# A chunked recurrence with inverses from GpSimd: ten units prepared ahead in place of eight, inverses returned in parts

## The chip, the cores and the metric

One core of a Trainium2 chip runs the whole program. The metric is the time of one execution in microseconds of device time, the median of several runs. TensorE multiplies matrices (stationary operand loaded first, results into PSUM), VectorE, ScalarE and GpSimd work elementwise, and SyncE's queue issues transfers; ScalarE's queue issues some too. Each engine works through its own list of instructions in order, and so does each queue: an instruction that waits holds up everything behind it.

## The reference

Two blocks follow each other. The first is a recurrence over 768 steps for 4 batches x 8 heads with a 40x40 state, the second a mixture of 8 experts with a capacity of 80 tokens each:

```python
for t in range(S):                                   # S = 768, D = 40, 32 chains (B x H)
    y[:, :, t] = einsum('bhd,bhde->bhe', r_t, state)
    Sa = einsum('bhde,bhe->bhd', state, a_t)
    state = state * w_t[:, :, None, :] - einsum('bhd,bhe->bhde', Sa, b_t) + einsum('bhd,bhe->bhde', v_t, k_t)
x = y.transpose(0, 2, 1, 3).reshape(B * S, H * D)    # 3072 tokens x 320
logits = x @ w_gate; expert = argmax(logits); gate = softmax(logits)[expert]
for e in range(8):                                   # the 80 tokens with the largest gate of each expert
    out[tok] = gate[tok] * (relu(x[tok] @ w1[e]) @ w2[e])
```

Everything is float32; w1 is 320x1024 and w2 is 1024x320 per expert. Tokens that are not kept stay zero.

## The kernel before

**Units and groups.** The 768 steps are cut into 12 chunks of 64. A unit is one chunk of two batches (16 chains), so there are 24 units, and batch pair 0 has the even ones, pair 1 the odd ones. Four units make a group (GU = 4, six groups). For a unit the 64 steps are solved at once: with N the strictly triangular 64x64 matrix of scores of each chain, the inverse of (I - N) is needed.

**prepare(n)** (line 356) loads w, a, k and b of a unit and makes what does not need the state: running products P of w and their inverses iv by two scans on VectorE (L374, L382), the scaled ah and kb (L392, L412), the transposed keys kbT (eight transposes on TensorE at L423, copied by ScalarE at L427), and two scores by TensorE at L438: N, which ScalarE copies to nt (L451), and Psi, which VectorE masks to psi (L455). LOOK = 8 rings of P, ah, kb and psi let units be prepared eight ahead of the solve; nt has two groups' worth.

**invert(gi)** (line 465) inverts the N of a group. Each 64x64 triangle is two 32x32 triangles and a 32x32 block below. out_go (L478) writes the triangles of the four units to `blocks` in device memory, fetch (L489) reads them back so that each of 128 partitions holds one 32x32 triangle (tile lt). 30 steps of two instructions (L497, L499) invert it in place: on VectorE for the first group, on GpSimd for the other five. end (L506, L507) closes it, flip (L511, GpSimd) makes the transposed copy ltT, two transfers (L517) put both to `solved` and `flipped`, and back_go (L522) reads them into nt, d1 and d0, eight transfers. lt and ltT have one buffer each.

**solve(n) and finish(n)** (lines 536, 570): two joins on TensorE (L546, L561) with copies by ScalarE (L551, L566) fill the lower block of the inverse. finish loads r and v (r on ScalarE's queue), transposes them, and does the products with the state: psi x V (L636), state x ah (L665), the inverse x W (L683, VectorE masks at L688), the keys' products (L705), the new state (L716, L725) and the tokens (L729, L739). Unit n+2 needs the state that unit n leaves.

**gate(gi)** (line 753) ranks the tokens of a group on VectorE, ten rounds of L807 and L808.

**What sets the order.** Nothing is scheduled at run time. Every piece is given to a Plan (line 18) with an engine, a duration, a lag, a due time, and the names that it reads and writes. Plan.order takes, again and again, the ready piece that can start first (within SLACK), and among those the one with the smaller key, ALPHA times the due time less the longest chain behind it; it assigns PSUM banks on the way. The list that comes out is emitted in that order, engine by engine, and stays fixed.

After the last unit the tops are merged (L828 on), the expert weights are loaded into the memory that the first part held, the chosen tokens are gathered and the experts computed (lines 830 to 1001).

## Time and profile before

| | |
|---|---|
| median of 3 runs | 606.74 us (604.84 to 608.82) |
| the profiled execution | 603.29 us, of it span 601.3 us |
| busy in the span: TensorE, VectorE, GpSimd, ScalarE | 424.1, 344.8, 248.5, 171.1 us |
| first join of the first group starts | 94.12 us |
| last token product of the first part | 464.57 us |
| the ranked tops are complete, the expert part starts | 478.9 us |
| TensorE's granted clock, mean | 0.848 of full speed |

The profiled execution lies 3.45 us under the median of the runs. The first part, up to 478.9 us, is what the change touches; the expert part takes the remaining 122 us. A stretch of the timeline in which TensorE has next to no busy time is one in which the whole chain waits, since the products with the state are all on TensorE.

### The profile page before, as it was taken

What the parts mean: (1) busy time and instruction counts of PE and PEld (TensorE: products, weight loads), DVE (VectorE), ACT (ScalarE), POOL (GpSimd) and SP (SyncE); (2) the same over time, 40 slices, a digit from 0 to 9 for tenths busy, and PEclk for the clock granted to TensorE, in tenths of its full rate; (3) what the DMA queues carried; (4) which work ended last, traced back from release to release, by engine and by line L of the source; (5) the groups of instructions that cost most, each with busy time, mean ns of one, the idle gap of its engine ahead of it and who ended that gap; (6) DMA issues with size and microseconds to landing.
All of it is one profiled execution on the core that took longest, in us unless ns stands there. A gap on an engine that the chain in (4) does not pass through costs nothing. (4 is left out here: it accounts for less than half of the span.)

```text
span 601.3 us, 20521 instructions
## 1 busy us (share of the span) xinstructions
PE 424.1 (71%) x8878; PEld 334.9 (56%) x8878; DVE 344.8 (57%) x692; ACT 171.1 (28%) x323; POOL 248.5 (41%) x392
## 2 busy tenths in 40 slices
PE   2853387998079975898559994984397104799996
PEld 1743266896068864787548883873286004244443
DVE  9985963795538763887546880764543883112121
ACT  1431142454024451444214542332042000110100
POOL 9010021798359860599518981388100002201011
PEclk9995687998579996999778995997599555699999
DMA  6586568556854558565593428414500299990000
GB/s 100 93 129 111 91 151 141 104 100 100 186 110 75 114 122 153 123 125 92 136 186 78 93 66 169 81 31 84 122 15 4 54 388 383 336 341 15 7 15 14
DMA packets 238414, 72.74 MB, mean 121 GB/s; under 512 B 218100, under 2 KB 232692, under 8 KB 238324
## 3 DMA queue, kind: packets, MB, share of 16 engines
q1 hardware_dynamic: 211444, 65.85, 48.2%
q10 hardware_dynamic: 26112, 3.94, 4.2%
q0 software_dynamic: 768, 1.64, 0.9%
q8 instruction: 70, 1.15, 0.8%
q14 instruction: 20, 0.16, 0.1%
HBM read 53.26 MB, written 18.13 MB: 119 GB/s over the span
## 5 line engine op out<-in xcount | busy, mean ns | idle before, releaser
L497 POOL TENSOR_TENSOR tmp<-lt 128x30 f32<-128x30 f32 (+9 forms) x150 | 89.0, 593 | 91.7 <-DMA lt<-blocks 80.3
L499 POOL TENSOR_TENSOR lt<-lt,tmp 128x30 f32<-128x30 f32 (+9 forms) x150 | 95.1, 634 | 11.8
L546 PE MATMUL ps<-d,nt 128*64 128x64 f32 x384 | 21.6, 273 | 52.8 <-DMA d<-flipped 52.8
L688 DVE TENSOR_TENSOR UL<-ps,mask 128x832 f32<-128x832 f32 x24 | 24.5, 1019 | 46.6 <-PE ps L683 46.4
L546 PEld LDWEIGHTS ps<-d,nt 128*64 128x64 f32 x384 | 18.8, 183 | 54.4 <-issue 40.7
L986 POOL DMA_INDIRECT out_dram<-y,idx_s x8 | 7.4, 921 | 74.4 <-DVE y L985 74.4
L438 PE MATMUL ps<-ah,kbT 40*64 40x64 f32 x1536 | 32.4, 231 | 7.8 <-ACT kbT L427 7.3
L427 ACT COPY kbT<-ps 128x1024 f32<-128x1024 f32 x24 | 24.3, 1013 | 43.7 <-PE ps L349 23.5
L983 PE MATMUL yp<-w,hT 128*80 128x320 f32 x128 | 35.9, 433 | 0.5 <-DVE hT L976 0.5
L438 PEld LDWEIGHTS ps<-ah,kbT 40*64 40x64 f32 x1536 | 27.9, 143 | 13.3 <-ACT kbT L427 9.7
L349 PE MATMUL ps<-ident,raww 128*128 128x128 f32 x96 | 18.3, 322 | 21.8 <-DMA raww<-in_w_dram 21.8
L716 DVE TENSOR_TENSOR st<-ps,st 128x832 f32<-128x832 f32 (+1 forms) x24 | 23.9, 995 | 16.3 <-PE ps L705 15.8
L455 DVE TENSOR_TENSOR psi<-ps,mask 128x512 f32<-128x512 f32 x24 | 16.1, 681 | 29.8 <-PE ps L438 29.7
L382 DVE TENSOR_TENSOR_SCAN iv<-dec,ends 128x520 f32<-128x520 f32 x24 | 31.4, 1309 | 2.6 <-ACT ivc L401 1.3
L374 DVE TENSOR_TENSOR_SCAN P<-dec,begins 128x520 f32<-128x520 f32 x24 | 31.8, 1323 | 1.4 <-ACT dec L370 1.1
L960 PE MATMUL hp<-w,xe 128*80 128x512 f32 x64 | 31.8, 643 | 0.5 <-DVE xe L952 0.5
L349 PE MATMUL ps<-ident,kb 128*128 128x128 f32 x192 | 27.7, 289 | 5.5 <-DVE kb L412 5.1
L739 PE MATMUL ps<-wsel,xT 128*128 128x88 f32 x192 | 27.0, 284 | 5.0 <-DVE xT L729 5.0
L592 ACT COPY rv<-ps 128x1024 f32<-128x1024 f32 x24 | 24.3, 1013 | 19.7 <-DMA rawr<-in_r_dram 9.7
L739 PEld LDWEIGHTS ps<-wsel,xT 128*128 128x128 f32 x192 | 23.6, 194 | 7.5 <-DVE xT L729 6.1
L551 ACT COPY gt<-ps 128x256 f32<-128x256 f32 x24 | 9.0, 374 | 66.2 <-PE ps L546 65.2
L485 POOL MEMSET nt<- 32x1024 f32 x12 | 11.3, 944 | 38.9 <-ACT nt L451 38.5
(157 smaller groups left out, 955.9 us busy)
## 6 DMA issues: line engine op xcount, KB each, us to landing
w<-in_moe_w_dram SPq DMA_DIRECT2D x8, 1280.0 KB
w<-in_moe_w_dram SPq DMA_DIRECT2D x8, 1024.0 KB, 14.3
x_rows<-xg SPq DMA_DIRECT2D x24, 160.5 KB, 3.2
rawkb<-in_k_dram SPq DMA_DIRECT2D x48, 80.0 KB, 3.0
rawkb<-in_b_dram SPq DMA_DIRECT2D x48, 80.0 KB, 2.9
raww<-in_w_dram SPq DMA_DIRECT2D x48, 80.0 KB, 3.2
rawa<-in_a_dram SPq DMA_DIRECT2D x48, 80.0 KB, 3.4
rawr<-in_r_dram ACTq DMA_DIRECT2D x96, 40.0 KB, 3.0
```

The lines of the kernel that those rows point to most:

```text
L349: nc.tensor.matmul(o, lhsT=i, rhs=ident, start=True, stop=True, is_transpose=True, skip_group_check=True)
L374: nc.vector.tensor_tensor_scan(at("P", n), at("dec", n)[:, 0 : H * SEG], begins, 0.0, op0=Alu.mult, op1=Alu.add)
L382: nc.vector.tensor_tensor_scan(at("iv", n)[:, H * SEG : 0 : -1], at("dec", n)[:, H * SEG : 0 : -1], at("ends", n)[:, H * SEG : 0 : -1], 0. ...
L427: nc.scalar.copy(at("kbT", n).rearrange("p (k c) -> p k c", k=2), ps[:, bank(kk) : bank(kk) + 2, :])
L438: nc.tensor.matmul(ps[T * o : T * o + T, b0 + q, T * m : T * m + T], lhsT=at("kbT", n)[rows, s0 : s0 + T], rhs=chain(at("ah", n), rows, m, ...
L497: e.tensor_tensor(out=tv, in0=t3[:, 0:s, s : s + 1].to_broadcast([128, s, n]), in1=t3[:, s : s + 1, s + 1 :].to_broadcast([128, s, n]), op ...
L499: e.tensor_tensor(out=t3[:, 0:s, s + 1 :], in0=t3[:, 0:s, s + 1 :], in1=tv, op=Alu.add)
L546: nc.tensor.matmul(ps[HB * q : HB * q + HB, b0, T * i : T * i + T], lhsT=nt[:, q, i, :], rhs=d0[:, q, i, :], start=True, stop=True, skip_g ...
L688: nc.vector.tensor_tensor(out=view(at("UL", n), 0, (M4 * X, 2), (1, M4 * X)), in0=view(ps[:, bank(ku), :], 0, (512, 2), (1, M4 * X)), in1= ...
L739: nc.tensor.matmul(ps[:, b0, 88 * m : 88 * m + 88], lhsT=at("xT", n)[:, 2 * T * cof(m, 0) : 2 * T * cof(m, 0) + 2 * T], rhs=wsel[:, m, :], ...
L960: nc.tensor.matmul(hp[j], lhsT=xe[:, i, :], rhs=w1[:, i, FH * j : FH * j + FH], start=i == 0, stop=False)
L983: nc.tensor.matmul(yp, lhsT=hT[:, f, :], rhs=w2[:, f, :], start=f == 0, stop=f == FK - 1)
```

## The change

- **Depth.** LOOK goes from 8 to 10, nt from two groups to three, lt from one buffer to two; psi shrinks from 8 buffers to 2, VL (the v tile) from 3 to 2. N and Psi are separated: the transposed keys are made as two halves, bT in prepare and kT in the new make_psi(n), which stands at the unit's solve.
- **Joins on 32-row tiles.** L546 and L561 multiplied 128-row operands whose other halves are zeros. Now only the 32-row blocks are multiplied, 16 matmuls in place of 8 for each join, each half into a PSUM bank of its own. The returned tiles d0 and d1 become one compact tile d, with no zeros to fill; the two fills of 128x2048 on GpSimd go.
- **The return in parts.** back_go becomes d0_go, d1_go and tm_go, three pieces on SyncE's queue with their own names (d0, d1, tm), so the first join needs d0, the second d1, and only the product with the inverse (L683) needs tm. There are still eight transfers. The clear of nt now stands behind the four units' N copies by name.
- **The flip** of an inverse moves from GpSimd to ScalarE.
- **Front.** The strict masks are copied by ScalarE (four copies) in place of VectorE (eight); loads of `a` for units 0 to 5 go through ScalarE's queue; the zero fills of padding get names of their own, so that the first loads don't stand behind them.
- **Order.** SLACK 0.15 to 0.05, ALPHA 0.5 to 0.25, and some of the durations that the Plan is told change by a few per cent.

```diff
-SLACK = 0.15
+SLACK = 0.05
-ALPHA = 0.5
+ALPHA = 0.25
...
-    LOOK = 8
-    RINGS = dict(dec=2, ..., psi=LOOK, nt=2 * GU, VL=3, UL=1, iv=1, ivc=1, ends=1, kbT=1, rv=1, lt=1, ltT=1, d0=GU, d1=GU, ...
+    LOOK = 10
+    RINGS = dict(dec=2, ..., psi=2, nt=3 * GU, VL=2, UL=1, iv=1, ivc=1, ends=1, bT=1, kT=1, rv=1, lt=2, ltT=1, tm=3 * GU, d0=GU, d1=GU, ...
-    WIDE = dict(nt=2, d0=1, d1=1)
+    WIDE = dict(nt=(3, GU * 512), d=(1, GU * 256))
...
-        for name in ("d0", "d1"):
-            for i, t in enumerate(wide[name]):
-                fill("POOL", t, 0.0, [(name, GU * i + u) for u in range(GU)], 2.0, -800.0)
...
-                for o in (0, X, 2 * X + D, 3 * X + D):
-                    nc.vector.tensor_copy(mask[rows, o : o + T], strict[rows, T * bb : T * bb + T])
+                for o in (view(mask[rows], 0, (X, 2), (1, T)), view(mask[rows], 2 * X + D, (X, 2), (1, T))):
+                    nc.scalar.copy(o, strict[rows, T * bb : T * bb + T].unsqueeze(1).to_broadcast([T, 2, T]))
...
-            load("rawa", n, z - 12, [(a, rows4)])
+            load("rawa", n, z - 12, [(a, rows4)], (), "ACT" if n < 6 else "SP")
...
+            key_turn(n, "bT", 1, z + 5)
+            kn = ("N", n)
+            add("PE", 0.62, 0.2, z + 7, score(n, kn, "bT", lambda q, bb: bb ^ q), ...)
...
+        def make_psi(n):
+            z = n * PER - 5
+            kp = ("Psi", n)
+            key_turn(n, "kT", 0, z)
+            add("PE", 0.62, 0.2, z + 1, score(n, kp, "kT", lambda q, bb: bb), ...)
...
             def flip():
-                nc.gpsimd.tensor_copy(at("ltT", kq)...
+                nc.scalar.copy(at("ltT", kq)...
-            add("POOL", 2.0, 0.1, z + 4.1, flip, [lk], [("ltT", kq)])
+            add("ACT", 1.05, 0.2, z + 4.1, flip, [lk], [("ltT", kq)])
...
-            add("SP", 4.8, 2.2, z + 5, back_go, [("sol", kq), ("flp", kq)], [(name, n) for n in ns for name in ("d0", "d1", "nt")])
+            add("SP", 1.2, 2.5, z + 4.4, d0_go, [("flp", kq)], [("d0", n) for n in ns])
+            add("SP", 2.2, 2.5, z + 4.5, d1_go, [("sol", kq)], [("d1", n) for n in ns])
+            add("SP", 1.1, 2.5, z + 4.6, tm_go, [("sol", kq)], [("tm", n) for n in ns], to=[("nt", n) for n in ns])
...
                 for i in range(M4):
                     for q in range(2):
-                        nc.tensor.matmul(ps[HB * q : HB * q + HB, b0, T * i : T * i + T], lhsT=nt[:, q, i, :],
-                                         rhs=d0[:, q, i, :], ...)
+                        for x in range(2):
+                            rows = slice(T * x, T * x + C)
+                            nc.tensor.matmul(ps[HB * q + C : HB * q + HB, b0 + x, C * i : C * i + C], lhsT=nt[rows, q, i, C:],
+                                             rhs=d0[rows, q, i, :], ...)
...
                 solve(n)
+                make_psi(n)
                 finish(n)
```

The order that the Plan makes of it is a table too long to show. Three places follow; numbers behind names are buffers.

GpSimd's list at the end of the second group's inversion (its lt is buffer 0 before, buffer 1 after); first before, then the change:

```order
L497 TENSOR_TENSOR tmp_150<-lt_0_129 128x30
L499 TENSOR_TENSOR lt_0_129<-lt_0_129,tmp_150 128x30
L195 AFFINE_SELECT lt_0_129<-lt_0_129 128x1024
L507 MEMSET lt_0_129 128x32
L511 COPY ltT_0_130<-lt_0_129 128x1024
L787 TENSOR_TENSOR ids_59<-gsm_0_145,tok_157 128x32
L788 COPY og_0_143<-gates_58 128x4x8
L485 MEMSET nt_0_146 32x32x32 x2
L497 TENSOR_TENSOR tmp_150<-lt_0_129 128x30
```

```order
L499 TENSOR_TENSOR tmp_151<-lt_1_130 128x30
L501 TENSOR_TENSOR lt_1_130<-lt_1_130,tmp_151 128x30
L195 AFFINE_SELECT lt_1_130<-lt_1_130 128x1024
L509 MEMSET lt_1_130 128x32
L487 MEMSET nt_2_149 32x32x32 x2
L499 TENSOR_TENSOR tmp_151<-lt_0_129 128x30
```

Between two inversions there stand two closing instructions and one clear, and the next inversion works on the other lt; the flip is gone from this list, and the ids of the first group come later.

SyncE's queue at the return of the second group's inverse (`solved`, `flipped`), with the fetch of the third group's triangles (lt<-blocks); first before, then the change:

```order
L517 DMA solved<-lt_0_129 128x1024
L795 DMA x_rows<-xg_0_137 64x2x321 x4
L517 DMA flipped<-ltT_0_130 128x1024
L478 DMA blocks<-nt_0_146 32x32x32 x4
L336 DMA VL_1_121<-in_v_dram 64x4x40 x4
L527 DMA nt_1_147<-solved 32x32x32
L529 DMA d1_0_149<-solved 32x16x32 x2
L527 DMA nt_1_147<-solved 32x32x32
L529 DMA d1_0_149<-solved 32x16x32 x2
L533 DMA d0_0_148<-flipped 32x32x32 x2
L489 DMA lt_0_129<-blocks 128x1024
```

```order
L519 DMA solved<-lt_1_130 128x1024
L480 DMA blocks<-nt_2_149 32x32x32 x4
L519 DMA flipped<-ltT_0_131 128x1024
L536 DMA d_0_150<-solved 32x16x32 x4
L491 DMA lt_0_129<-blocks 128x1024
L529 DMA d_0_150<-flipped 32x32x32 x2
L541 DMA nt_1_148<-solved 32x32x32 x2
```

The tokens (x_rows) and the v tile (VL) no longer stand inside the return, and the fetch comes ahead of the last four transfers. The fetches of the second, fourth and sixth group's triangles stand ahead of `solved` of the group before; that of the fifth stands inside the return again.

VectorE's list inside the first group's inversion, after the change:

```order
L501 TENSOR_TENSOR lt_0_129<-lt_0_129,tmp_151 128x13x18
L374 SCALAR_TENSOR_TENSOR P_8_96<-dec_0_79,begins_152 128x520
L499 TENSOR_TENSOR tmp_151<-lt_0_129 128x238
L501 TENSOR_TENSOR lt_0_129<-lt_0_129,tmp_151 128x14x17
L625 TENSOR_TENSOR VL_0_120<-ps_78,mask_153 128x2x4x64
L499 TENSOR_TENSOR tmp_151<-lt_0_129 128x240
L501 TENSOR_TENSOR lt_0_129<-lt_0_129,tmp_151 128x15x16
L378 RECIPROCAL ends_0_125<-P_8_96 128x8
L499 TENSOR_TENSOR tmp_151<-lt_0_129 128x240
L501 TENSOR_TENSOR lt_0_129<-lt_0_129,tmp_151 128x16x15
L382 SCALAR_TENSOR_TENSOR iv_0_123<-dec_0_79,ends_0_125 128x520
```

Work of units 6 to 9 and of the first solves now stands between the steps: four L412, two L374, two L382, two L378, two L392, two L625 and one L457 in all. Before, one L412 stood between the steps.

## Rows read from the trace of the kernel before

**Rows 1.** Busy time by stretch: bounds, length, engines, granted TensorE clock, DMA share, GB/s
```profile
53.02:75.53 22.51, 10.18 (x100) 8.45 (x100) 20.52 (x62) 3.20 (x4) 0.00 (x0) 0.58 0.56 87
...
94.12:149.20 55.08, 51.58 (x1336) 45.52 (x1336) 37.73 (x54) 24.25 (x45) 36.99 (x60) 0.91 0.61 112
149.20:168.85 19.65, 0.47 (x1) 0.21 (x2) 8.66 (x32) 0.91 (x2) 5.71 (x8) 0.57 0.85 174
168.85:223.10 54.25, 51.28 (x1404) 45.07 (x1404) 38.27 (x53) 26.11 (x48) 42.82 (x66) 0.97 0.48 102
...
231.87:295.90 64.03, 57.97 (x1478) 50.07 (x1478) 46.73 (x87) 26.23 (x49) 43.42 (x67) 0.90 0.59 121
...
305.01:359.90 54.89, 51.86 (x1368) 45.83 (x1368) 40.26 (x60) 23.36 (x43) 41.42 (x63) 0.93 0.47 95
...
369.72:412.80 43.08, 40.62 (x1169) 36.39 (x1169) 24.87 (x52) 16.93 (x34) 27.37 (x47) 0.91 0.36 69
412.80:431.43 18.63, 0.67 (x12) 0.22 (x2) 9.71 (x35) 0.23 (x1) 9.79 (x21) 0.55 0.68 151
431.43:465.70 34.27, 29.70 (x888) 26.35 (x888) 14.55 (x24) 11.47 (x24) 0.00 (x0) 0.94 0.05 9
465.70:478.92 13.22, 0.47 (x2) 0.21 (x2) 10.77 (x44) 0.74 (x3) 0.45 (x2) 0.51 0.19 50
```

**Rows 2.** The same view, over three of GpSimd's five inversions (columns as above)
```profile
107.58:149.41 41.83, 39.30 (x1096) 34.66 (x1094) 31.61 (x47) 20.19 (x34) 37.13 (x61) 0.96 0.55 96
...
313.66:357.18 43.52, 41.62 (x1120) 37.00 (x1118) 34.88 (x49) 20.30 (x36) 38.82 (x61) 0.96 0.37 74
383.87:420.15 36.28, 26.66 (x823) 23.67 (x812) 22.54 (x51) 12.03 (x25) 31.58 (x61) 0.93 0.30 54
```

**Rows 3.** SyncE's queue in order of time: start us, issue us, line, transfer, count
```profile
150.92 0.35 SPq L517 DMA_DIRECT2D solved<-lt  x1
...
154.96 4.06 SPq L478 DMA_DIRECT2D blocks<-nt  x4
...
166.45 0.64 SPq L489 DMA_DIRECT2D lt<-blocks  x1
```

**Rows 4.** VectorE in order of time, the front: start us, us, line, operation
```profile
3.06 8.87 DVE L281 COPY mask<-strict 64x64 f32<-64x64 f32 x8
...
13.26 1.24 DVE L374 TENSOR_TENSOR_SCAN P<-dec,begins 128x520 f32<-128x520 f32 x1
```

**Rows 5.** ScalarE in order of time, the front
```profile
8.66 0.59 ACT L370 COPY dec<-ps 128x512 f32<-128x512 f32 x1 [6.56 <-PE ps L349]
```

**Rows 6.** SyncE's queue in order of time, the front
```profile
3.63 2.67 SPq L333 DMA_DIRECT2D raww<-in_w_dram  x4
...
39.83 2.51 SPq L478 DMA_DIRECT2D blocks<-nt  x4
...
48.06 0.54 SPq L489 DMA_DIRECT2D lt<-blocks  x1
```

**Rows 7.** DMA issues: transfer, count, KB each, median us from issue to landing
```profile
lt<-blocks SPq DMA_DIRECT2D x6, 512.0 KB, 4.9
solved<-lt SPq DMA_DIRECT2D x6, 512.0 KB, 3.0
...
d<-flipped SPq DMA_DIRECT2D x12, 128.0 KB, 2.5
```

**Rows 8.** Groups by line and shape: busy us, mean ns; idle us before them, releaser
```profile
L438 PE MATMUL ps<-ah,kbT 40*64 40x64 f32 x1536 | 32.4, 231 | 7.8 <-ACT kbT L427 7.3 <-issue 0.3
...
L374 DVE TENSOR_TENSOR_SCAN P<-dec,begins 128x520 f32<-128x520 f32 x24 | 31.8, 1323 | 1.4 <-ACT dec L370 1.1
L382 DVE TENSOR_TENSOR_SCAN iv<-dec,ends 128x520 f32<-128x520 f32 x24 | 31.4, 1309 | 2.6 <-ACT ivc L401 1.3
...
L546 PE MATMUL ps<-d,nt 128*64 128x64 f32 x384 | 21.6, 273 | 52.8 <-DMA d<-flipped 52.8
...
L412 DVE TENSOR_TENSOR kb<-rawkb,ps 128x640 f32<-128x640 f32 x24 | 19.6, 815 | 7.6 <-PE ps L349 7.1 <-DMA rawa<-in_a_dram 0.4
```

More of the change, by code (lines that the diff above doesn't have):

```diff
@@ L222 @@
         buf = {n: [hold.tile([128, COLS[n]], F32, name=f"{n}_{i}") for i in range(RINGS[n])] for n in COLS}
-        wide = {n: [hold.tile([128, GU * 512], F32, name=f"{n}_{i}") for i in range(WIDE[n])] for n in WIDE}
+        wide = {n: [hold.tile([128, cols], F32, name=f"{n}_{i}") for i in range(k)] for n, (k, cols) in WIDE.items()}
         tmp = hold.tile([128, C * C // 4], F32, name="tmp")
@@ L240, in group @@
         def group(name, n):
-            return wide[name][(n // GU) % WIDE[name]]
+            return wide[name][(n // GU) % WIDE[name][0]]
         def quads_of(name, n, rows=slice(0, 128)):
@@ L276, in consts, with masks @@
             nc.vector.memset(begins[:, ::SEG], 1.0)
+        def masks():
             nc.vector.memset(mask, 1.0)
@@ L336, in go @@
                             q.dma_start(to[:, g], s[:, M4 * g : M4 * g + M4])
-            add(eng, (2.4 if name in ("rawr", "VL") else 1.3) * len(parts), 2.2, when, go, reads, [(name, n)])
+            add(eng, (2.8 if name in ("rawr", "VL") else 1.3) * len(parts), 3.0, when, go, reads, [(name, n)])
         def rows3(t, o=0):
@@ L452, in prepare, with key_turn, turn_go, score @@
             add("ACT", 0.6, 0.2, z + 8, nt_go, [kn], [("nt", n)])
+        def key_turn(n, name, x, z):
+            kk = (name + "p", n)
+            def turn_go():
+                for m in range(M4):
+                    turn(ps[:, bank(kk), 128 * m : 128 * m + 128], at("kb", n)[:, 512 * x + 128 * m : 512 * x + 128 * m + 128])
+            add("PE", 0.53, 0.2, z, turn_go, [("kb", n), ("kbpad", n % RINGS["kb"])], (), (kk, 1), [(name, n)])
+            add("ACT", 0.59, 0.2, z + 1, lambda: nc.scalar.copy(at(name, n), ps[:, bank(kk), :]), [kk], [(name, n)])
+        def score(n, key, name, half):
+            def go():
+                b0 = bank(key)
+                for m in range(M4):
+                    for q, bb in halves:
+                        rows = slice(HB * q, HB * q + D)
+                        o = half(q, bb)
+                        s0 = 128 * m + T * bb
+                        nc.tensor.matmul(ps[T * o : T * o + T, b0 + q, T * m : T * m + T],
+                                         lhsT=at(name, n)[rows, s0 : s0 + T],
+                                         rhs=chain(at("ah", n), rows, m, bb), start=True, stop=True, skip_group_check=True)
+            return go
+        def quads(key):
+            return ps[:, bank(key) : bank(key) + 2, 0:256]
+        def make_psi(n):
+            z = n * PER - 5
+            kp = ("Psi", n)
+            key_turn(n, "kT", 0, z)
+            add("PE", 0.62, 0.2, z + 1, score(n, kp, "kT", lambda q, bb: bb), [("kT", n), ("ah", n)], (), (kp, 2), [("psi", n)])
             def psi_go():
@@ L485, in clear @@
                     nc.gpsimd.memset(nt[T * x + C : T * x + T, :, 0:C], 0.0)
-            add("POOL", 2.4, 0.1, z, clear, (), [("nt", n) for n in ns])
+            add("POOL", 2.4, 0.1, z, clear, [("nt", n) for n in ns], [("tm", n) for n in ns])
             def fetch():
@@ L718, in sum_go @@
                         in1=view(st, o, (BS, M4), (step, 2), (1, n_)), op=Alu.add)
-            add("DVE", 0.7 if last else 1.03, 0.2, z + 0.9, sum_go, [ky], [old, y0])
+            add("DVE", 0.7 if last else 1.06, 0.2, z + 0.9, sum_go, [ky], [old, y0])
             if not last:
```

126 lines of the change are left out of this document (54 added, 72 removed).

## The prediction, written before the changed kernel ran

> **What bounds the kernel now.** I read busy time by stretch first, cut where TensorE starts and stops, because the chain of waits ends in the expert part and says nothing of the first 479 us. TensorE works in six stretches, one per group, with nearly nothing between them [rows 1]: 55.08, 54.25, 64.03, 54.89, 43.08 and 34.27 us, together 305.60. Between their bounds lie five holes of 19.65, 8.77, 9.11, 9.82 and 18.63 us, together 65.98. Ahead of the first stretch are 94.12 us, behind the last 13.22 us of ranking.
>
> What ends a hole is a returned inverse. The inversions take 41.83 to 43.52 us for four groups and 36.28 us for the last [rows 2] (the first, the fourth and the fifth stand there). So GpSimd works some 43 us per group against TensorE's 54: the slower engine is not the bound, the latency around it is. In [rows 3] SyncE puts an inverse out at 150.92, then issues other transfers, and serves the fetch of the next triangles at 166.45. The hole ends at 168.85 [rows 1]. The reader should see two things: a finished inverse needs 18 us to become work for TensorE, and GpSimd gets its next input only after that.
>
> **The front.** VectorE's mask copies hold it for 8.87 us from 3.06, and the first scan starts at 13.26 [rows 4], though its input was copied by 8.66 + 0.59 = 9.25 [rows 5]. The first w load was issued at 3.63 [rows 6] and now leads the queue, some 2.8 us sooner. With the copies on ScalarE the scan can start at 9.25 - 2.8 = 6.45, that is 6.8 us sooner. The triangles went out from 39.83 to 42.34 and their fetch was issued at 48.06 [rows 6]; with a landing of 3 us, as for the larger put [rows 7], it could go at 45.5, so I take 2.5 us there. Against this, the first inversion, 22.51 us on VectorE [rows 1], now has other work between its steps: four scans at 1.323 and 1.309 [rows 8] are 5.3 us, eight more instructions at no more than 0.815 [rows 8] are at most 6.5, less the one that stood there: 11.0 us. (Two reciprocals of 8 columns are left out.) It ends at 75.53 - 6.8 - 2.5 + 11.0 = 77.2. The return took 18.59 us (94.12 less 75.53, [rows 1]). The two landings that it can't avoid are 3.0 + 2.5 [rows 7]; between 5.5 and 18.59 I take 10.5, nearer the lower end, because tokens and v tiles no longer stand in it. First join: 87.7 in place of 94.12, **-6.4 us**. Bounds: -12 (no more between two landings), and +8 if a step's neighbour waits for a load as the fetch did, 48.06 less 39.83.
>
> **The holes.** The second group's fetch now stands ahead of the first return, so GpSimd starts its inversion at about 80 in place of 107.58 (its list holds it only until the first inversion, over at 77.2, is closed by two instructions). Five inversions at 4 x 43 + 36.28 are 208. Between them stand a clear, or, for the third and fifth group, a fetch behind a put (blocks, landing, fetch, 4.9 us landing [rows 7]); I take 4 and 11 us, together 30, where before it was up to 22 each (149.41 to 171.45 and so on). The last inverse is done at 318 and returned at 328.7. TensorE's path: 87.7 plus the six stretches, about 295 (below), is 383. Laid side by side, inverses land near 133.5, 187.5, 234.5, 288.5 and 329; TensorE, at the stretches' lengths less the 10.0 that its first one loses (below), asks for them near 133, 187, 251, 305 and 348. Two come just in time, three early. So the holes close, and TensorE's own work becomes the end: **-66 us**. I don't believe all of it. Each list is fixed, and SyncE must now issue the same transfers in less time with two v tiles in place of three. A return can find TensorE waiting for anything between 0 and the smallest hole, 8.77; I take 2 us for each of five, nearer to none since GpSimd's path is ahead: **+10 us**.
>
> **Inside the stretches.** Two more units are prepared before the first join. A stretch with four prepares takes 54.25, the last, with none, 34.27 [rows 1]: at most 5.0 us per prepare, -10.0. Psi moves to the solve; units 0, 1 and 2 have it by then, eight had it before, so five more fall inside: a score is 32.4 / 48 = 0.675 us [rows 8] and its transposes no more, +6.8. The joins: 21.6 / 24 = 0.90 us for 8 matmuls of 128 rows [rows 8]; the nearest row for 16 small-tile matmuls is the score at 0.675. The 48 joins thus cost between -11 and, were each half as dear again, +21; I take 0. Granted clock: in the holes it is 0.55 to 0.57 [rows 1], in the stretches 0.90 to 0.97. At half speed for twice the missing share, that costs (0.09 x 55 + 0.03 x 54 + 0.10 x 64 + 0.07 x 55 + 0.09 x 43 + 0.06 x 34) = 22.8 us; without holes I take a third back, **-8**. Sum: 305.6 - 10.0 + 6.8 + 0 - 8 = 294.4, **-11.2 us**.
>
> The flip on ScalarE, the fills that go and the compact tile are off the path: GpSimd has 29 us in hand (below), and ScalarE was busy 26.11 of 54.25. Without that cover the flip's place in the return is the one that counts, and it lies in the 10.5.
>
> **The sum.** -6.4 - 66 + 10 - 11.2 = -73.6 us. The profiled execution took 603.29 (span 601.3), so 529.7; the median shown is 3.45 higher, so **533 us**.
>
> **The rivals.**
>
> *Half of the waiting stays.* The lists were made with other durations than the chip's, and every return still finds TensorE waiting for about 9 us. For it: no hole before was under 8.77, and SyncE's order still has the fifth group's fetch inside a return. Against it: GpSimd starts 27 us sooner and the fetch is ahead in three of five groups. 45 us in place of 10 gives 568. Chance 0.17.
>
> *The lock makes GpSimd the bound, and the kernel slower.* GpSimd's path is 80 + 208 + 30 + 10.5 + 34.27 + 13.22 = 376; TensorE's with tail and the 10 is 405. So an inversion may grow by 29 / 5 = 5.8 us before it decides, and at 43 + 21.9 = 65 us the first part ends 6 us later than 478.92: slower by 1%, 613. For it: with VectorE busy 22.54 of 36.28 us (0.62) an inversion took 36.28, with 34.88 of 43.52 (0.80) it took 43.52 [rows 2], 7.2 us for 0.18 more; and the change packs both engines closer. Against it: carried on to a VectorE that never rests this adds 8 us, 51.5 in all, and the path is then 376 + 40 = 416, 541 to 544 us in all and far from slower. The Trainium skill ("SBUF — State Buffer", Who interferes with whom) says that a VectorE instruction with two SBUF inputs and a GpSimd instruction that reads SBUF lock each other out for a whole instruction, whichever starts second. By that rule GpSimd's steps, which all read SBUF, stretch further as VectorE's scans and token products crowd in; the trace agrees in direction, 36.28 against 43.52. Chance of slower by over 1%: 0.05, with what else I don't see.
>
> *It gives more.* No return waits (-10), joins at the score's price (-11), the clock's other half (-7): 505 us. Chance 0.10.
>
> *It doesn't do what it says.* The later reads wait on names that the buffers tie together: d is one buffer, so a return waits for the last second join of the group before, and everything behind it on SyncE too. If that keeps the holes whole and the front ends at its bound of +8, -11 + 8 is left, 604 us, within 1% of before. [rows 3] shows that order holding the fetch by 15 us; against it, the joins of a group's last unit stand well ahead of the next return. Chance 0.04.
>
> **How the numbers follow.** My forecast, 515 to 555, has 0.64, half of the waiting 0.17, more 0.10, no change 0.04, slower 0.05. A measurement of this kernel tells about 1% from no change. Faster by over 1%: 0.91; within: 0.04; slower: 0.05. The range takes the forecast's own, more than half of the quick case and more than half of the 568 case: 506 to 570. It is the sum's -27 (front -6, no waits -10, joins -11) and +37 (joins +21, front +14, and some clock).
>
> **What would show it.** The first join near 88 and the second group's inversion starting near 80; five holes of under 4 us; the fourth inversion starting within 5 us of the third's end; inversions of 43 to 48 us; the ranked tops near 405 in place of 478.9; the expert part unchanged at 122 us. The forecast is wrong if the waiting in front of the first join line is still 9 us per group, if an inversion takes over 49 us, or if TensorE's stretches stay at 55 to 64 us without holes, since then waits inside them have taken the place of those between.

## The result: faster, by less than a third of what was forecast

The changed kernel takes 582.91 us (median of four, 575.81 to 585.08) beside 605.79 for the kernel before in the same runs: a ratio of 0.958, interval 0.948 to 0.968. The ratio leaves out executions that ran slower than the others (here the one of 585.08 us; further down also one of 1040 us, in the run with the old numbers and large matmuls, whose cause no trace shows), the median keeps them. The forecast was 533 (506 to 570). The direction is right, the size is not. In the profiled executions (603.29 and 582.16 us) the ranked tops come at 458.26 in place of 478.92; the expert part takes 122 us as before. So 20.7 of the 21.1 us lie in the first part.

### The profile page after: what moved, and what is told of

Same layout as the page of the kernel before. It is cut to its first block, busy times and chain, and to the rows that moved or that the text cites. A ratio compares the mean times of both kernels' runs of the same rounds, so it can differ in the third digit from the quotient of the medians.

```text
span 580.4 us, 22119 instructions
## 1 busy us (share of the span) xinstructions
PE 445.7 (77%) x9646; PEld 351.8 (61%) x9646; DVE 320.7 (55%) x684; ACT 186.4 (32%) x357; POOL 224.1 (39%) x385
## 3 DMA queue, kind: packets, MB, share of 16 engines
q10 hardware_dynamic: 32448, 4.92, 5.6%
## 5 line engine op out<-in xcount | busy, mean ns | idle before, releaser
L499 POOL TENSOR_TENSOR tmp<-lt 128x30 f32<-128x30 f32 (+9 forms) x150 | 86.4, 576 | 59.4 <-DMA lt<-blocks 48.3
L501 POOL TENSOR_TENSOR lt<-lt,tmp 128x30 f32<-128x30 f32 (+9 forms) x150 | 89.3, 595 | 11.8
L349 PE MATMUL ps<-ident,kb 128*128 128x128 f32 x192 | 35.0, 316 | 6.9 <-DVE ends L378 4.0
L560 PE MATMUL ps<-d,nt 32*32 32x32 f32 x768 | 14.4, 211 | 32.5 <-DMA d<-flipped 32.1
L487 POOL MEMSET nt<- 32x1024 f32 x12 | 11.3, 946 | 63.1 <-ACT nt L422 62.8
L374 DVE TENSOR_TENSOR_SCAN P<-dec,begins 128x520 f32<-128x520 f32 x24 | 30.8, 1287 | 5.6 <-ACT dec L370 5.5
L412 DVE TENSOR_TENSOR kb<-rawkb,ps 128x640 f32<-128x640 f32 x24 | 19.5, 814 | 24.6 <-PE ps L349 17.6
L560 PEld LDWEIGHTS ps<-d,nt 32*32 32x32 f32 x768 | 10.8, 122 | 36.8 <-DMA d<-flipped 23.2
L732 DVE TENSOR_TENSOR st<-ps,st 128x832 f32<-128x832 f32 (+1 forms) x24 | 23.9, 995 | 16.5 <-PE ps L721 15.0
L755 PE MATMUL ps<-wsel,xT 128*128 128x88 f32 x192 | 28.8, 298 | 3.3 <-DVE xT L745 1.9
L349 PEld LDWEIGHTS ps<-ident,kb 128*128 128x128 f32 x192 | 23.8, 158 | 11.3 <-issue 6.3
L382 DVE TENSOR_TENSOR_SCAN iv<-dec,ends 128x520 f32<-128x520 f32 x24 | 29.9, 1247 | 0.8 <-ACT ivc L401 0.5
L755 PEld LDWEIGHTS ps<-wsel,xT 128*128 128x128 f32 x192 | 25.6, 208 | 5.2 <-DVE xT L745 2.3
L983 ACT ACTIVATE h<-hp 80x512 f32<-80x512 f32 x16 | 8.6, 588 | 61.2 <-PE hp L980 61.2
L1000 PEld LDWEIGHTS yp<-w,hT 128*80 128x80 f32 x128 | 18.5, 150 | 14.8 <-issue 0.8
L652 PE MATMUL ps<-VL,psi 64*64 64x104 f32 x768 | 26.2, 282 | 0.1
```

Of the source, the lines that this page charges most:

```text
L349: nc.tensor.matmul(o, lhsT=i, rhs=ident, start=True, stop=True, is_transpose=True, skip_group_check=True)
L374: nc.vector.tensor_tensor_scan(at("P", n), at("dec", n)[:, 0 : H * SEG], begins, 0.0, op0=Alu.mult, op1=Alu.add)
L382: nc.vector.tensor_tensor_scan(at("iv", n)[:, H * SEG : 0 : -1], at("dec", n)[:, H * SEG : 0 : -1], at("ends", n)[:, H * SEG : 0 : -1], 0. ...
L499: e.tensor_tensor(out=tv, in0=t3[:, 0:s, s : s + 1].to_broadcast([128, s, n]), in1=t3[:, s : s + 1, s + 1 :].to_broadcast([128, s, n]), op ...
L501: e.tensor_tensor(out=t3[:, 0:s, s + 1 :], in0=t3[:, 0:s, s + 1 :], in1=tv, op=Alu.add)
L560: nc.tensor.matmul(ps[HB * q + C : HB * q + HB, b0 + x, C * i : C * i + C], lhsT=nt[rows, q, i, C:], rhs=d0[rows, q, i, :], start=True, st ...
```

## The profile after

First the busy time by stretch, cut as in [rows 1]: bounds, length, then busy us and instruction counts of TensorE, its weight loads, VectorE, ScalarE and GpSimd, then TensorE's granted clock, DMA share, GB/s. The first row is the inversion on VectorE, the second the return of its result.

```profile
51.17:91.79 40.62, 25.60 (x399) 20.92 (x397) 30.33 (x76) 12.25 (x19) 1.89 (x2) 0.73 0.74 115
91.79:105.23 13.44, 0.00 (x1) 0.00 (x1) 0.00 (x0) 1.93 (x2) 11.65 (x25) 0.56 0.83 199
105.23:151.40 46.17, 41.48 (x1256) 36.64 (x1256) 29.13 (x37) 20.15 (x39) 27.68 (x42) 0.91 0.45 85
151.40:159.22 7.82, 0.04 (x4) 0.03 (x1) 1.60 (x5) 0.85 (x1) 0.75 (x3) 0.73 1.09 211
159.22:220.62 61.40, 56.34 (x1477) 48.62 (x1477) 40.64 (x79) 27.71 (x52) 43.34 (x77) 0.87 0.69 136
220.62:223.23 2.61, 0.00 (x1) 0.03 (x1) 2.61 (x4) 0.16 (x1) 2.30 (x5) 0.99 1.14 180
223.23:281.64 58.41, 55.43 (x1480) 48.29 (x1480) 29.85 (x45) 25.79 (x49) 33.31 (x50) 0.82 0.63 124
...
282.59:354.01 71.42, 66.39 (x1670) 57.60 (x1670) 51.13 (x108) 30.14 (x55) 52.27 (x90) 0.81 0.57 116
...
354.53:402.47 47.94, 45.20 (x1405) 40.37 (x1405) 31.47 (x80) 19.74 (x37) 21.52 (x40) 0.89 0.41 83
...
403.44:445.00 41.56, 35.44 (x1205) 31.04 (x1205) 23.90 (x61) 15.51 (x33) 0.46 (x2) 1.00 0.23 43
```

Read it in three parts. **The holes** are 7.82, 2.61, 0.95, 0.52 and 0.97 us, together 12.87 where [rows 1] had 65.98. **The front** is longer: the first join comes at 105.23, not at 94.12. **The stretches** are longer too: 326.9 us together against 305.6, although two units fewer are prepared in them. The last column but two says where to look: the granted clock is 0.81 to 0.91 in five of them, where it was 0.90 to 0.97. The formula of the prediction, missing share times length, gives 4.2 + 8.0 + 10.5 + 13.6 + 5.3 + 0 = 41.5 us for these stretches against 22.8 before. 11.1 - 53.1 + 21.3 = -20.7 us.

Next, what TensorE does behind a return, in order of time (start us, us, line, operation, count, idle before it). First the changed kernel, behind the hole that ends at 223.23:

```profile
223.23 0.28 PE L560 MATMUL ps<-d,nt 32*32 32x32 f32 x2 [2.61 <-DMA d<-flipped]
223.94 0.65 PE L560 MATMUL ps<-d,nt 32*32 32x32 f32 x30 [0.42 <-DMA d<-flipped]
224.51 2.01 PE L755 MATMUL ps<-wsel,xT 128*128 128x88 f32 x8
226.45 1.67 PE L652 MATMUL ps<-VL,psi 64*64 64x104 f32 x32
228.04 1.08 PE L577 MATMUL ps<-d,gt 32*64 32x32 f32 x32
...
230.11 0.65 PE L560 MATMUL ps<-d,nt 32*32 32x32 f32 x32
```

Then the kernel before, behind the hole that ends at 231.87:

```profile
231.87 1.12 PE L546 MATMUL ps<-d,nt 128*64 128x64 f32 x16 [8.79 <-DMA d<-flipped]
232.92 1.12 PE L349 MATMUL ps<-ident,st 128*128 128x128 f32 x4
233.97 1.13 PE L438 MATMUL ps<-ah,kbT 40*64 40x64 f32 x32
...
235.44 1.12 PE L561 MATMUL ps<-d,gt 128*64 128x64 f32 x16
236.35 1.07 PE L546 MATMUL ps<-d,nt 128*64 128x64 f32 x16
```

And the same stretches as windows, the changed kernel:

```profile
223.23:227.30 4.07, 3.65 (x60) 3.29 (x64) 0.95 (x2) 0.89 (x3) 3.68 (x6) 0.50 0.31 49
231.40:235.50 4.10, 4.10 (x54) 3.19 (x53) 0.17 (x1) 2.16 (x4) 2.78 (x5) 0.50 0.58 161
235.50:240.40 4.90, 4.90 (x130) 4.58 (x127) 2.16 (x7) 1.15 (x3) 0.32 (x2) 0.51 0.21 32
240.40:244.50 4.10, 4.10 (x141) 3.57 (x140) 3.11 (x4) 0.98 (x2) 3.71 (x6) 1.00 0.48 89
```

and the kernel before:

```profile
231.87:237.40 5.53, 5.53 (x89) 4.62 (x89) 2.06 (x6) 1.17 (x3) 0.00 (x0) 0.51 0.54 123
237.40:241.50 4.10, 3.71 (x126) 3.31 (x126) 3.89 (x14) 1.25 (x4) 0.00 (x0) 1.00 1.08 166
```

Both come out of the hole at 1.2 GHz. Before the change TensorE is back at 2.4 GHz after 5.5 us; after it, it is busy but for 0.42 us and needs 17 (of all returns the one with the longest such stretch; all are compared below). Of these 17 us it spends 11.8 on tiles of at most 64 rows, 3.3 on transposes and 2.0 on the token products with 128 rows (L755); of the 5.5 before the change, 3.4 are products with 128 rows. The same product (L652, 32 of 64x104) takes 1.67 us in this stretch and 0.94 at full clock. The two lists differ in more than one thing; what the change itself made smaller is the joins' tiles, and that their size matters is the theory that the experiments try.

To compare whole kernels I split the time from the first join to the end of the last token product into three: idle time, work at full clock, and what half clock adds. "At half clock" is busy time times twice the missing share of the clock, summed over windows of half a microsecond; half of it is lost. Before: 371.6 = 87.4 idle + 262.4 work + 21.8 lost (43.6 at half clock). After: 339.8 = 39.4 + 260.3 + 40.0 (79.9). The work is the same, 48 us of idle time went, and 18 came back through the clock.

## The experiments

All figures of the split come from one profiled execution each, and ratios are to the kernel before in the same runs. Two executions of one program (below) differed by 15 us in work at half clock, so a smaller difference tells nothing.

| kernel | us, ratio (interval) | first join | idle | work | at half clock |
|---|---|---|---|---|---|
| before | | 94.12 | 87.4 | 262.4 | 43.6 |
| changed | 582.9, 0.958 (0.948 to 0.968) | 105.23 | 39.4 | 260.3 | 79.9 |
| large matmuls at returns | 576.7, 0.951 (0.940 to 0.962) | 107.36 | 27.5 | 279.9 | 42.2 |
| the same, small | 592.0, 0.975 (0.969 to 0.981) | 107.79 | 27.0 | 277.2 | 82.9 |
| before, small joins alone | 614.1, 1.013 (1.007 to 1.019) | 91.76 | 78.1 | 255.4 | 100.3 |
| eight ahead | 614.2, 1.016 (1.007 to 1.025) | 91.77 | 78.0 | 264.9 | 80.9 |
| eight ahead, large joins | 611.3, 1.008 (1.004 to 1.012) | 96.64 | 81.5 | 267.4 | 62.9 |
| one triangle tile | 590.0, 0.971 (0.959 to 0.982) | 105.14 | 44.7 | 256.0 | 90.6 |
| first inversion whole | 573.9, 0.944 (0.933 to 0.955) | 92.65 | 47.1 | 262.1 | 67.5 |
| old numbers of the order | 587.4 (573.6 to 588.9) | 86.89 | 40.7 | 266.4 | 112.0 |
| old numbers, large matmuls | 582.2, 0.957 (0.947 to 0.967) | 90.61 | 34.5 | 288.0 | 66.8 |
| both mendings, four matmuls | 570.6, 0.942 (0.935 to 0.949) | 97.37 | 37.0 | 281.0 | 36.5 |
| both, eight | 578.4, 0.951 (0.942 to 0.960) | 100.80 | 30.2 | 297.2 | 31.4 |
| both, two | 569.1, 0.939 (0.931 to 0.947) | 95.59 | 38.9 | 272.5 | 48.1 |
| both, two, again | 572.9, 0.936 (0.930 to 0.942) | 95.08 | 38.7 | 270.3 | 63.1 |

### Does the size of the tiles hold the clock down?

Large matmuls ahead of each group's first join, in the changed kernel:

```diff
+                if n % GU == 0:
+                    for _ in range(4):
+                        nc.tensor.matmul(ps[:, b0, 0:512], lhsT=ident, rhs=at("kb", n)[:, 0:512], ...)
```

> The changed kernel with four more matmuls of 128 rows by 512 columns (of no use to the result) ahead of each group's first join, which wait for no return. Theory: after a return TensorE runs on tiles of 32 to 64 rows and keeps the granted clock of 0.5 for 9.6, 17.2 and 14 us of nearly unbroken work (from 159.2, 223.2 and 283.4), where before the change, with joins on 128 rows, 3.6 to 5.7 us were enough; in all some 85 us of its work ran at half clock, against 42 before. Large tiles ahead of the joins then bring the clock back within 6 us of a return: half-clock work falls to 50 us or less, which gives 15 to 18 us back for 24 matmuls of 0.6 to 1.2 us (14 to 29 us, of which the holes of 13 us hide a part): the time is between 570 and 585. Rival: the clock is low because of the pauses, not because of the tile sizes; then the clock returns no sooner after the first join and the time grows by the matmuls, to 592 to 605.

The control: the same columns, on a corner of the array. The two lists are the same but for these rows.

```diff
-  ps[:, b0, 0:512], lhsT=ident, rhs=at("kb", n)[:, 0:512]
+  ps[0:C, b0, 0:512], lhsT=ident[0:C, 0:C], rhs=at("kb", n)[0:C, 0:512]
```

> The changed kernel with the same four extra matmuls of 512 columns ahead of each group's first join, of the same count, place and length in columns as in the run with large ones, but on a corner of 32 rows by 32 columns of the array. In that run the work at half clock between the first join and the end of TensorE's part fell from 79.9 to 42.2 us. Theory: the size of the tiles decides; small ones do not bring or keep the clock up, half-clock work stays at 70 us or more, and the extra columns cost their time: 585 to 600 us, slower than both the changed kernel (583) and the run with large ones (577). Rival: any unbroken work holds the clock; then this run does as well as the large ones: 42 to 50 us at half clock and about 577 us.

With large ones 576.7 us and 42.2 us at half clock, with small ones 592.0 and 82.9: as the theory had it, and the rival of "any unbroken work" falls. The intervals of these two are apart (that of the large ones overlaps the changed kernel's). The same return shows it, in order of time on TensorE and in windows. Large:

```profile
223.89 3.60 PE L558 MATMUL ps<-kb,ident 128*128 128x512 f32 x8
227.95 0.24 PE L564 MATMUL ps<-d,nt 32*32 32x32 f32 x2 [0.45 <-DMA d<-flipped]
```

```profile
227.95:232.00 4.05, 3.43 (x122) 3.02 (x125) 1.11 (x4) 1.04 (x4) 3.58 (x7) 1.00 0.49 77
...
236.00:240.40 4.40, 4.40 (x154) 3.93 (x157) 2.98 (x8) 1.07 (x4) 3.25 (x8) 1.00 0.73 181
```

Small:

```profile
223.75 3.62 PE L558 MATMUL ps<-kb,ident 32*32 32x512 f32 x8
228.04 0.31 PE L564 MATMUL ps<-d,nt 32*32 32x32 f32 x2 [0.67 <-DMA d<-flipped]
```

```profile
228.04:232.00 3.96, 3.56 (x56) 3.21 (x60) 0.09 (x1) 0.89 (x3) 3.49 (x7) 0.50 0.51 80
...
236.00:240.40 4.40, 4.40 (x59) 3.49 (x57) 0.23 (x2) 2.31 (x5) 1.73 (x4) 0.50 0.42 130
```

Same place, same 3.6 us of matmuls, a wait of 0.45 and 0.67 us behind them; the clock stays at 2.4 GHz in one and falls to 1.2 in the other. The large ones did not hold it everywhere: behind the first two returns, after waits of 10.7 and 3.6 us, it was back only 11.3 and 8.8 us after the first join. For its second part the expectation was off: the large matmuls cut the number of falls, from nine spells at half clock to six, more than they shortened each.

The joins alone, in the kernel before (its padded tiles kept, only the 32-row blocks multiplied):

```diff
-  nc.tensor.matmul(ps[HB * q : HB * q + HB, b0, ...], lhsT=nt[:, q, i, :], rhs=d0[:, q, i, :], ...)
+  for x in range(2):
+      rows = slice(T * x, T * x + C)
+      nc.tensor.matmul(ps[HB * q + C : HB * q + HB, b0 + x, ...], lhsT=nt[rows, q, i, C:],
+                       rhs=d0[rows, q, i, C * x : C * x + C], ...)
```

> The kernel before the change with one part of the change alone: the joins on 32-row tiles (sixteen matmuls in place of eight, in two banks of PSUM in place of one, which also moves some steps in the order). Theory: small tiles at a return keep TensorE at half clock: in the kernel before, 29.7 us of its work ran at half clock right after the six returns, 43.6 us in all between the first join and the end; with small joins it is 60 to 75 us in all, and since the joins themselves are cheaper (14.4 and 20.5 us busy against 21.6 and the like), the time rises by 5 to 12 us: 610 to 618. Rival: holes of 9 to 20 us are what drops the clock there and any work brings it back; half-clock work stays below 50 us and the time falls with the cheaper joins, 598 to 605.

It came out as the theory had it in sign, and the half-clock work rose further than expected, from 43.6 to 100.3 us. A stretch behind a return at 230.98, in windows:

```profile
235.00:239.00 4.00, 4.00 (x129) 3.61 (x128) 3.67 (x12) 0.75 (x2) 0.00 (x0) 0.50 0.62 103
...
247.00:251.00 4.00, 4.00 (x74) 3.55 (x73) 3.66 (x11) 1.47 (x5) 2.19 (x8) 0.55 0.11 24
251.00:255.00 4.00, 4.00 (x123) 3.53 (x125) 1.30 (x2) 2.23 (x3) 3.45 (x8) 1.00 0.10 15
```

Some 20 us at half clock, where the same return in the kernel before (231.87, above) had 5.5. This one part of the change makes the kernel before slower by 1.3% (0.7 to 1.9), with less work in it (255.4 us against 262.4). Its order moved too, since the joins take two banks each.

### Is it the depth that closes the holes?

```diff
-    LOOK = 10
+    LOOK = 8
```

> The changed kernel with units prepared eight ahead in place of ten, all else kept. Theory: the rings of three triangle groups and two inverse tiles, not the depth of ten, let GpSimd start early; the holes stay at about 13 us in all and the time within 8 us of 583, and the front is shorter by two units' preparing (first join 5 us sooner). Rival: the depth closes the holes; with eight each return finds TensorE waiting 5 us or more again, holes of 30 to 60 us, 600 us or more.

Its rival holds: 614.2 us, idle time 78.0 in place of 39.4. Depth is worth all of the gain; the rest of the change without it is slower than before, by 1.6% (0.7 to 2.5). The front, though, is 13.5 us shorter (91.77).

With the joins on 128 rows, as before the change, on top of that (the joins' and returns' lines of the kernel before, each waiting for the whole return):

> The kernel of the run with eight ahead, with the joins as they were before the change: 128-row tiles on inverses padded with zeros (eight matmuls per join in place of sixteen; the padded tiles take the room that ten ahead would need). To be compared with the run with eight ahead and compact tiles. Theory: the small tiles keep the clock down; with large ones the clock is back within 3.6 to 6 us of each return, TensorE's work at half clock falls by 25 to 40 us and the time by 10 us or so, although a join then costs 0.90 us in place of 0.60 (48 of them, +14 us at most). Rival: the clock does not depend on the joins; the time rises by up to 14 us, or stays.

The time moved by about 3 us, less than expected, with intervals that overlap; 80.9 to 62.9 us at half clock is little more than two executions of one program differ. Behind the returns themselves it is plain. I take TensorE's busy time from a group's first join, or from the clock's fall where that comes up to 3 us later, until the clock is back, over every return at which it was down. With large joins that is 3.1 to 7.5 us in the kernel before and 3.0 to 5.7 in this run; with small ones it is 7.7 to 16.6 in the changed kernel, 9.5 to 18.4 in the kernel before with small joins alone, and 9.3 to 16.5 with eight ahead. Windows from a group's first join (the first row) and over a whole spell at half clock, small joins:

```profile
91.77:102.40 10.63, 9.25 (x264) 8.26 (x268) 1.79 (x2) 2.49 (x6) 9.45 (x16) 0.50 0.18 29
224.62:242.40 17.78, 17.17 (x421) 14.76 (x425) 12.53 (x36) 4.08 (x11) 0.00 (x0) 0.52 0.62 111
```

and large ones:

```profile
96.64:100.20 3.56, 3.10 (x51) 2.81 (x51) 0.00 (x0) 0.74 (x2) 3.17 (x6) 0.51 0.02 5
229.80:233.40 3.60, 3.14 (x66) 2.87 (x65) 0.42 (x2) 1.12 (x3) 0.00 (x0) 0.53 0.66 139
```

One tile for the triangles in place of two, ten ahead kept:

```diff
-  lt=2
+  lt=1
```

> The changed kernel with one tile for the triangles being inverted in place of two: a group's fetch must wait until the inverse before it is put out, as it did before the change; ten ahead and the rest are kept. Theory: the depth of ten closes the holes (with eight they were open again, 614 us), and the tile only saves GpSimd the fetch; its idle time between inversions grows by some 8 us per group, but it has time in hand, so the holes grow by less than 10 us in all: 583 to 592. Rival: the early fetch is what closes them; without it each return is late by 8 us or more, holes of 40 to 60 us, 605 to 625.

590.0 us, within the theory: idle time grew by 5 us only, and the interval overlaps the changed kernel's. The early fetch, on which the prediction leaned, is worth little beside the depth.

### What made the front longer?

The first inversion whole, by the lag that the order counts between its steps:

```diff
-  add(eng, us, 0.1, z + s * 0.1, step, ...)
+  add(eng, us, 0.05 if on_vector else 0.1, z + s * 0.1, step, ...)
```

> The changed kernel with one number of the order changed: the steps of the first inversion, on VectorE, count 0.05 us of lag between them in place of 0.1, so that the order no longer puts other work between them (two products of kb stay there, of the 16 scans, products and masks). In the changed kernel that inversion lasted from 51.17 to 91.79, 40.6 us, against 22.51 before. Theory: the front is late by what stands between the steps and by the loads that this work waits for (the wait of 4.92 us on TensorE, which waited 5.36 us for a w tile). Then the inversion takes 24 to 26 us, the first join comes near 90 in place of 105.2, and since TensorE's own work sets the end, the ranked tops come 10 to 15 us sooner: about 570 us in all against 583. Rival: the ten units must be prepared anyway; what stood between the steps now stands behind them, the first stretch grows by what the front loses, and the time stays within 4 us of 583.

The inversion took 23.1 us (51.90 to 75.03) in place of 40.62, the first join came at 92.65, and the time is 573.9: the theory, nearly in full. Of the 17.5 us, 4.2 went again in the return, whose order also moved, and 0.7 in a later start. In the changed kernel the rows that cost the time are these, on VectorE, then on TensorE (start us, us, line, operation, wait before it):

```profile
30.77 0.82 DVE L412 TENSOR_TENSOR kb<-rawkb,ps 128x640 f32<-128x640 f32 x1 [2.65 <-DMA rawkb<-in_b_dram]
...
51.17 0.19 DVE L499 TENSOR_TENSOR tmp<-lt 128x30 f32<-128x30 f32 x1 [1.36 <-DMA lt<-blocks]
...
85.22 0.82 DVE L412 TENSOR_TENSOR kb<-rawkb,ps 128x640 f32<-128x640 f32 x1 [4.92 <-PE ps L349]
```

```profile
80.15 1.09 PE L349 MATMUL ps<-ident,raww 128*128 128x128 f32 x4 [5.36 <-DMA raww<-in_w_dram]
```

A product that was put between two steps waits for TensorE, which waits for a w tile; the next step of the inversion stands behind it.

The two numbers of the order set back:

```diff
-SLACK = 0.05      ALPHA = 0.25
+SLACK = 0.15      ALPHA = 0.5
```

> The changed kernel with the two numbers of the order that the change lowered set back (slack 0.15 in place of 0.05, weight of the due times 0.5 in place of 0.25), all else kept. In its order only two products stand between the steps of the first inversion, and more weight on the due times lets early units go first. Theory: the front alone differs, as in the run without work between the steps; first join near 92, holes as in the changed kernel, 570 to 576 us. Rival: the lower numbers also closed the holes (triangles ahead of solves); with the old ones the returns are late again, idle time behind the first join goes from 39 us to 60 or more, and the time is 590 to 605.

No verdict: its runs lie between 573.6 and 588.9 us. The holes stay closed (idle 40.7), so the rival falls, and the first join comes 18 us sooner, but 112.0 us ran at half clock. That split is of an execution of 587.4 us; the fastest, of 573.6, lies within the theory and has no profile. With four large matmuls at the returns as well:

> The changed kernel with the two numbers of the order set back and with four large matmuls ahead of each group's first join. With the old numbers alone the first join came at 86.89, idle time behind it was 40.7 us, but 112.0 us of TensorE's work ran at half clock, and the time was 587. Theory: that time was lost to the clock alone; large tiles cut the half-clock work to 45 us or less, and with the sooner front the time is 560 to 568, below the 570.6 of the run with both. Rival: the half-clock work there follows pauses inside the stretches, which matmuls at the returns don't touch; it stays above 70 us and the time is 578 to 590.

582.2 us: half-clock work fell to 66.8, between the two expectations, while work grew by 22 us. Why the old order held more work at half clock, and whether it does in every execution, is not settled.

### The mendings together

> The changed kernel with both: no work between the steps of the first inversion, and four large matmuls ahead of each group's first join. Alone the first gave 573.9 us (the first join at 92.65 in place of 105.23), the second 576.7. Theory: one acts ahead of the first join and the other behind it, so the gains of 9 and 6 us add: 566 to 570 us. Rival: the large matmuls gained by filling idle time that a sooner start has already moved elsewhere (idle time behind the first join grew from 39.4 to 47.1 us there); then the time is that of the first alone, 572 to 576.

570.6 us: between the two. It is 12 us below the changed kernel, with intervals that just touch; against the first inversion alone the intervals overlap. Two large matmuls in place of four, and eight:

> The run with both, with two large matmuls ahead of each group's first join in place of four. Four cost some 22 us of TensorE's time at full clock (282.1 against 260.3 of work) and left 36.4 us at half clock. Theory: as many are needed as fill a return's wait and bring the clock up; two are too few, half-clock work goes back to 55 us or more, and the time is 572 to 577. Rival: two suffice, and 11 us of work are saved: 560 to 566.

> The run with both, with eight large matmuls ahead of each group's first join in place of four. Theory: four already hold the clock at the returns; the other 24 matmuls cost 0.6 us each, 14 us, less what lies in waits: 575 to 583. Rival: the clock at 36.4 us of half-clock work still has something to give; half-clock work falls under 20 us and the time stays at 567 to 573.

569.1 us with two, between its theory and its rival, and 578.4 with eight: eight cost their work, as expected (297.2 us), and from four to two no loss can be seen. Once more, in five rounds:

> The fastest version so far (the first inversion whole, two large matmuls ahead of each group's first join) measured once more in more rounds. Theory: its 569.1 us holds: 566 to 572, a ratio to the kernel before of 0.93 to 0.945 and below that of the changed kernel (0.958, interval 0.948 to 0.968). Rival: it was a lucky placing of the clock; then it comes out with the first inversion alone, at 573 to 578.

572.9 us, a ratio of 0.936 (0.930 to 0.942). It beats both kernels, the one before by 6%. That the large matmuls add to the first inversion whole (0.944, 0.933 to 0.955) is not shown by the times. Nor is it by the split: work at half clock was 48.1 us in the first profile of this program and 63.1 in the second, beside 67.5 without the matmuls.

### Is GpSimd late as well?

The ranking's two small products moved off GpSimd, in the changed kernel and in the mended one:

```diff
-  nc.gpsimd.tensor_tensor(out=ids[...], ...);  nc.gpsimd.tensor_copy(og[...], gates[...])
+  nc.vector.tensor_tensor(out=ids[...], ...);  nc.vector.tensor_copy(og[...], gates[...])
```

> The changed kernel with the two small products of a group's ranking (token numbers and gates) on VectorE in place of GpSimd. In the changed kernel they stood inside two of GpSimd's inversions and waited there for VectorE: 5.64 us in the one from 214 and 9.68 + 1.21 us in the one from 341, and 3.3 us behind the last token product. Theory: TensorE's own work, half of its lateness by its clock, sets the end, and GpSimd has that time to spare; only the 3 us at the end come back: 578 to 582. Rival: GpSimd's chain is as late as TensorE's (its inversions take 227.5 us with 67.6 us between them, from 93.2 on); then 13 us less in it lets two returns come earlier and the time falls to 565 to 572.

> The fastest version so far (first inversion whole, two large matmuls ahead of each group's first join; 569.1 and 572.9 us) with the two products of the ranking on VectorE. Theory: 3 us at the end come back: 566 to 570. Rival: with the front and the clock mended GpSimd's chain is what is late, and the inversions freed of these waits give 8 us or more: 558 to 564.

593.8 us (0.974, 0.969 to 0.979) and 573.2 (0.945, 0.939 to 0.950). The first is slower than the changed kernel, and neither expectation held: work at half clock came out at 90.3 us and idle time at 46.6; the order of everything had been worked out anew. The second decides nothing: its executions lie between 562.6 us, within the rival, and 577.5, above both. Whether GpSimd's list sets the remaining idle time stays open.

## Why the prediction was wrong

The sum's terms, forecast and measured in the profiled executions: **front** -6.4, +11.1; **holes** -66 + 10, -53.1; **inside the stretches** -11.2, +21.3. Together -73.6 and -20.7.

**The holes were right in size, the mechanism named for it was not.** 12.87 us are left where 10 were forecast. But the second group's inversion began at 93.20, not at 80, 67.5 us lie between the inversions, not 30, and the last ended at 388.20, not at 318. Windows over GpSimd's five inversions, columns as above:

```profile
93.20:132.50 39.30, 25.63 (x736) 22.80 (x736) 17.06 (x21) 12.95 (x24) 34.66 (x61) 0.74 0.50 109
158.32:205.57 47.25, 42.15 (x1110) 36.79 (x1110) 30.86 (x64) 19.31 (x38) 37.03 (x65) 0.82 0.69 125
214.06:262.20 48.14, 44.28 (x1113) 38.12 (x1102) 30.87 (x46) 19.44 (x40) 37.91 (x62) 0.82 0.61 116
288.49:333.90 45.41, 43.62 (x1066) 38.09 (x1060) 34.85 (x68) 20.72 (x41) 39.40 (x64) 0.82 0.46 84
340.78:388.20 47.42, 42.17 (x1158) 37.64 (x1159) 29.37 (x77) 15.49 (x30) 31.96 (x62) 0.82 0.39 78
```

The pauses ahead of the third and the fifth group are 25.8 and 26.3 us, where 11 were forecast; GpSimd waits there for the fetch of triangles. It was not ahead by the 29 us of the forecast; both lists were late together. That the holes came out near 10 us is luck in part. The runs with eight ahead and with one tile show that depth closes the holes and the early fetch hardly matters.

**The clock failed**, the step "without holes I take a third back, -8". It cost 18.7 us more instead of 8 less, 27 us off. The step took the loss to follow the holes (and read their clock as 0.55 to 0.57, which holds for the two longest; in the other three it was 0.66 to 0.73). What the runs show is that the clock fell at short pauses as well (2.61 us ahead of 223.23; 0.95 us ahead of 282.59, with the fall two microseconds behind it; but not at the 0.97 us ahead of 403.44), and that it was back later where the joins ran on small tiles. How much of the loss the joins' size makes in the changed kernel itself is not measured: ten ahead with 128-row joins was not run. The trace of before had a sign of it: the clock came back behind 128-row joins, and these very joins were to become 32-row tiles. I priced them by their duration alone ("The 48 joins thus cost between -11 and, were each half as dear again, +21; I take 0."). In duration the first join did get cheaper, from 21.6 us [rows 8], and the second, L561 with 20.1 us before, stayed the same:

```profile
L560 PE MATMUL ps<-d,nt 32*32 32x32 f32 x768 | 14.4, 211 | 32.5 <-DMA d<-flipped 32.1 <-issue 0.3
L577 PE MATMUL ps<-d,gt 32*64 32x32 f32 x768 | 20.5, 247 | 2.2 <-issue 1.7 <-ACT gt L565 0.5
```

The rest of the stretches came to +2.6 us against a forecast of -3.2. One of the prediction's own signs of being wrong came true with it: without holes, the stretches still last 41.56 to 71.42 us.

**The front failed** in its three steps. The start: the first scan did begin 5.8 us sooner (7.50 for 13.26), but the inversion only 1.9 us sooner (51.17 for 53.02), not 9.3. Up to the fetch VectorE was busy for 31.52 us where before it had 41.45, with the DMA engines at 0.81 in place of 0.66: it waited for loads, as at 30.77 above. So the lead shrank on the way: the first N was copied 4.2 us sooner, the fourth, which completes the group, only 1.1 us (35.12 for 36.18), and its triangles went out until 42.46 for 42.34.

```profile
0.00:46.81 46.81, 25.70 (x348) 21.39 (x348) 31.52 (x60) 18.02 (x34) 12.95 (x34) 0.88 0.81 118
```

The interleaving: 11.0 us were forecast for the work between the steps, 18.1 came (40.62 less 22.51). The trace has 16 pieces there, with three L625 in place of the two of the list; their durations add up to 12.7 us, near the forecast, and four of them waited, for 8.7 us in all (0.71, 1.22, 1.82 and 4.92). I counted the durations of what is put between and not what each piece waits for. The return: 10.5 forecast, 13.44 measured; the first put stood behind other transfers on SyncE's queue and went out at 96.30, 3.0 us after the closing. 7.4 + 7.1 + 2.9 make the 17.5 us.

**The rivals.** Half of the waiting did not stay, more did not come, and the kernel did get faster. GpSimd's steps did not get longer: 576 and 595 ns on the average, against 593 and 634 before.

```profile
L499 POOL TENSOR_TENSOR tmp<-lt 128x30 f32<-128x30 f32 (+9 forms) x150 | 86.4, 576 | 59.4 <-DMA lt<-blocks 48.3
L501 POOL TENSOR_TENSOR lt<-lt,tmp 128x30 f32<-128x30 f32 (+9 forms) x150 | 89.3, 595 | 11.8
```

The inversions of 45 to 48 us are long because other instructions wait inside them, one of them for VectorE's ranking (start us, us, line, wait):

```profile
372.76 0.24 POOL L803 TENSOR_TENSOR ids<-gsm,tok 128x32 f32<-128x32 f32 x1 [9.68 <-DVE gsm L794]
```

The rival's condition did not come about: VectorE was busy for 0.43 to 0.77 of an inversion in the windows above, never more than the 0.80 of [rows 2]. So the rule of the Trainium skill ("SBUF — State Buffer", Who interferes with whom), from which it took that closer packing stretches GpSimd's steps, was not put to the test here.

## What to carry to other kernels

When a matmul is cut to its non-zero blocks, look at the granted clock behind each wait, not at the duration alone: here the smaller joins left TensorE less work and made the kernel before 1.3% slower. What is put between the steps of a critical chain brings its own waits into the chain, so price it by what it waits for. And do not count on the clock coming back when a hole shrinks: here it fell at a pause of 0.95 us too.

## What the runs showed of the hardware that I had not expected

- TensorE, busy mostly on tiles of 32 and 64 rows (11.8 us, with 3.3 of transposes and 2.0 of token products between), stayed at 1.2 GHz for 17 us in the changed kernel (223.2 to 240.3, with one pause of 0.42); with 128-row joins it was back at 2.4 GHz after 3.0 to 5.7 us of work (the run with eight ahead and large joins).
- Eight records of 512 columns on 32x32 of the array took 3.62 us, on 128x128 3.60 us; behind the latter the clock stayed up at this return, behind the former it fell.
- The Trainium skill ("TensorE: Matmul & The Clock Gate", Part 1) says that activity releases the throttle. If busy time is what is meant, the run with small matmuls does not agree: TensorE was busy for all but 0.4 us from 228.04 to 240.40 and the clock was 0.50. In the run with large ones it was no busier, and the clock stayed at 1.00 from 227.95 to 240.40.
